# Attention inside one core: the order of TensorE's products, with V-products in groups of three and two, nine P tiles, and seven PSUM banks shared by name

## The chip, the cores and the metric

The kernel runs on one core of one Trainium2 chip. The metric is the device time of one execution in microseconds (us); lower is better. Several executions are timed and the median is given. One execution is also recorded by the hardware profiler; its rows are what this text quotes.

## What is computed

One transformer block for 2048 tokens of width 448: a layer norm with a condition, attention with 16 heads of 28 columns, a residual sum, a second layer norm, and a gated MLP that mixes over tokens. Only the attention matters here:

```python
qkv = (lambda x, *d: x.transpose(*d))((x @ wqkv).reshape(B, S, 3, H, Dh), 2, 0, 3, 1, 4)
q, k, v = qkv[0], qkv[1], qkv[2]
scores = jnp.einsum("bhqd,bhkd->bhqk", q, k) * (Dh ** -0.5)
p = _softmax(scores, axis=-1)
o = jnp.einsum("bhqk,bhkd->bhqd", p, v)
```

with B = 1, S = 2048, H = 16, Dh = 28, all in float32.

## The kernel before

The order of the instructions on each engine is the order in which the code writes them; nothing reorders it later. Tiles come from pools, and an instruction that takes a tile waits until the readers of the tile's last use are done.

A head is worked in 16 key tiles of 128 keys. Three kinds of TensorE (PE) instructions alternate:

- **S products** (`s_mm`, L637): the scores of one key tile against 512 queries, into a PSUM bank; four to a key tile, 64 to a head. ScalarE (ACT) reads each bank and writes the exponential into a P tile (L641). A P tile holds two such results, so a key tile takes two P tiles.
- **M products** (`m_mm`, L607): the same scores laid out the other way, one query tile against 512 keys, 20 tiles (`LEAD`) ahead of the S products. VectorE (DVE) reduces each bank to its row maximum (L612). The maxima of a head are gathered by `m_max` (three small DVE operations, L618, L620, L85), transposed by PE in `m_fin` (L626), copied by DVE (L628), and sent by DMA into two spare rows of the head's queries, so that a later S product already holds the score less its maximum.
- **V products** (`pv_mm`, L652): P times V for one key tile. The four query blocks go to four column strips of the array, into one PSUM bank `o_ps`, the same for a whole head. After the last key tile of a head DVE copies `o_ps` out (`n_copy`, L661); the sums then travel by DMA, DVE takes their reciprocal (L671), and GpSimd (POOL) multiplies.

A slot `u` is one key tile: four S products and four M products in turn, S first. After every second slot come the V products of the two key tiles before. Work of other kinds hangs on slots in a table, `events`: head loads, copies, DMAs, the preparation of weights for later stages (`ws_*`, `wo_*`, `wout_*`). It is issued at the start of its slot.

Of the eight PSUM banks seven are handed out by `bank()`. In the attention loop three of them (tag `s`) belong to S products, four (tag `m`) to M products and to the transpose in `m_fin`; each kind goes round its own banks. The eighth is `o_ps`. Six P tiles go round.

So a stretch of S and M products without V products in between (a *run* below) is 16 products long, and after it PE does the V products of two key tiles (a *group* below).

Of the kernel before, what the change touches and what calls it, by code (L numbers as in the profile page):

```python
# [8 lines left out]
F32 = mybir.dt.float32  # L9
F32R = mybir.dt.float32r  # L10
# [6 lines left out]
S, D, H, DH, FH = 2048, 448, 16, 28, 896  # L17
EPS = 1e-5
SCALE = DH ** -0.5
NT = S // 128  # L20
# [13 lines left out]
def tile_adaln_mha_gmlp(ctx, tc, x, wqkv, wo, w_in, w_spT, b_sp, w_out, cT, w_mod, out):  # L34
    nc = tc.nc
    ctx.enter_context(tc.manual_schedule())
    pe, dve, act, pool, sp = nc.tensor, nc.vector, nc.scalar, nc.gpsimd, nc.sync

    const = ctx.enter_context(tc.tile_pool(name="const", bufs=1))
    dpool = ctx.enter_context(tc.tile_pool(name="dpool", bufs=1, side="right"))  # L40
# [22 lines left out]
    heapD = [dpool.tile([128, n * 896], F32R, name=f"heapD{i}", tag=f"heapD{i}") for i, n in enumerate((8, 8, 4))]  # L63
# [3 lines left out]
    def hview(heap, off, a, b):  # L67
        return heap[:, off : off + a * b].rearrange("p (a b) -> p a b", b=b)
# [3 lines left out]
    class Halves:  # L72


        def __init__(self, n, lo, hi):
            self.n, self.views = n, (lo, hi)
# [7 lines left out]
    def sub(eng, dst, a, hi):  # L84
        eng.tensor_tensor(out=dst, in0=a, in1=hi.bitcast(F32), op=ALU.subtract)  # L85
# [5 lines left out]
    def weight_part(dst, i, raw, hi_eng, lo_eng, zero=True, c0=0):  # L91

        cs = slice(c0, c0 + raw.shape[-1])
        h = dst[:, i if i < 3 else 6, cs]
        if hi_eng is act:
            act.activation(h, raw, AF.Copy)
        else:
            hi_eng.tensor_copy(h, raw)
        if i < 3:
            sub(lo_eng, dst[:, 3 + i, cs], raw, h)  # L100
        else:
            sub(lo_eng, dst[0:64, 7, cs], raw[0:64], h[0:64])
            if zero:
                pool.memset(dst[64:128, 7, cs].bitcast(F32), 0.0)
# [37 lines left out]

    ps = ctx.enter_context(ExitStack())
    ring = ps.enter_context(tc.tile_pool(name="ring", bufs=1, space=PSUM))
    turn = [0]
    ps_o = ps.enter_context(tc.tile_pool(name="ps_o", bufs=1, space=PSUM))

    att = ctx.enter_context(ExitStack())
# [15 lines left out]
    def bank(name, kind=None):  # L164

        if kind is None:
            kind = "smsmsmm"[turn[0] % 7]
            turn[0] += 1
        return ring.tile([128, 512], F32, name=name, tag=kind, bufs=3 if kind == "s" else 4)

    def load_mod(pair, eng):
        for k in range(4):
# [413 lines left out]

    ppool = att.enter_context(tc.tile_pool(name="ppool", bufs=6))

    class Slots:


# [3 lines left out]
            return heapD[n][p, o : o + c.stop - c.start]  # L595

    OT = Slots()
    wos = hview(heapD[2], 0, 8, D)

    pms = {}  # L600

    steady = []

    def m_mm(j, kb):
        h, t = divmod(j, NT)
        mt = bank("mt", *steady)
        pe.matmul(  # L607
            mt, qst[h % 3][:, t * 128 : (t + 1) * 128], kst[h % 3][:, kb * 512 : (kb + 1) * 512], start=True, stop=True
        )
        if h not in pms:  # L610
            pms[h] = npool.tile([128, NT, 4], F32, name="pm")
        dve.tensor_reduce(out=pms[h][:, t, kb : kb + 1], in_=mt, axis=AX.X, op=ALU.max)  # L612
# [3 lines left out]
    def m_max(h):  # L616
        nm = npool.tile([128, NT], F32, name="mxv")
        dve.tensor_reduce(out=nm, in_=pms.pop(h), axis=AX.X, op=ALU.max, negate=True)  # L618
# [4 lines left out]
    def m_fin(h):  # L623
        mx = mxs.pop(h)
        tp = bank("mtp", *steady)
        pe.transpose(tp[0 : 2 * NT, 0:128], mx.bitcast(F32), ident)  # L626
        nf = npool.tile([2 * NT, 128], F32, name="nf", bufs=1)
        dve.tensor_copy(nf, tp[0 : 2 * NT, 0:128])  # L628
# [5 lines left out]
    def s_mm(u, qb):  # L634
        h, kt = divmod(u, NT)
        st = bank("st_ps", "s" if u + LEAD < NU else None)
        pe.matmul(st, kst[h % 3][:, kt * 128 : (kt + 1) * 128], qst[h % 3][:, qb * 512 : (qb + 1) * 512], start=True, stop=True)  # L637
        if qb % 2 == 0:
            ptiles[u, -1] = ppool.tile([128, 2, 512], F32, name="P")
        p = ptiles[u, -1][:, qb % 2, :]  # L640
        act.activation(p, st, AF.Exp, scale=SCALE)  # L641
        ptiles[u, qb] = p
# [4 lines left out]
    def pv_mm(u):  # L647
        h, kt = divmod(u, NT)
        if kt == 0:
            otile[h] = ps_o.tile([128, 512], F32, name="o_ps", tag="o")  # L650
        for qb in range(4):
            pe.matmul(  # L652
                otile[h][32 * qb : 32 * qb + 32, :], V[:, kt, h, :], ptiles.pop((u, qb)), start=kt == 0, stop=kt == NT - 1
            )
# [3 lines left out]
    def n_copy(h):  # L658
        osb[h] = stage.tile([128, 512], F32, name="osb", tag="qf")
        if h < H - 1:  # L660
            dve.tensor_copy(osb[h], otile.pop(h))  # L661
        else:
            act.activation(osb[h], otile.pop(h), AF.Copy)
# [47 lines left out]
    wo_raw = {}  # L711
# [7 lines left out]

    def wo_prep(i):  # L720
        pool.tensor_tensor(out=wo_raw[i], in0=wo_raw[i], in1=bcs["ga"], op=ALU.mult)
        weight_part(wos, i, wo_raw.pop(i), pool, pool)

    wout_t = {}

# [58 lines left out]

    LEAD = 20
    NU = H * NT
    events, late = {}, {}

    def at(slot, fn, *a, when=events):
        when.setdefault(slot, []).append((fn, a))  # L790

    for h in range(H):
        if h >= 2:
            at(h * NT - LEAD - 10, load_head, h)
        e0 = (h + 1) * NT
        at(e0 + 1, n_copy, h)
# [5 lines left out]
        at(h * NT + NT - LEAD, m_max, h)  # L802
        at(max(h * NT + NT - LEAD, -2), m_fin, h, when=late)
# [17 lines left out]

# [20 lines left out]
    steady.append("m")  # L842
    for u in range(NU + 1):
        for fn, a in events.pop(u, []):
            fn(*a)
        j = u + LEAD
        for qb in range(4 if u < NU else 0):
            s_mm(u, qb)
            if j < NU:
                m_mm(j, qb)  # L850
        if u % 2 == 0 and u > 0:
            pv_mm(u - 2)
            pv_mm(u - 1)
        for fn, a in late.pop(u, []):
            fn(*a)
    tail_events = {fn.__name__: [(fn, a)] for k in sorted(events) for fn, a in events[k]}

    def run_tail(*names):
# [23 lines left out]
    def wo_mm(t, steps):  # L882
        if t not in wo_ps:
            wo_ps[t] = bank("wo_ps") if t % 8 < 7 else ps_o.tile([128, 512], F32, name="wo_ps", tag="o")
        for a, b in steps:
            pe.matmul(  # L886
                wo_ps[t][:, :D],
                OT[:, a, t * 128 : (t + 1) * 128],
                wos[:, b, :],
                start=(a, b) == STEPS[0],  # L890
                stop=(a, b) == STEPS[-1],
            )
# [50 lines left out]
    def wo_tile(t):  # L943
        wo_mm(t, STEPS)
        wo_add(t)
# [36 lines left out]
    for t in range(1, HELD):  # L982
        wo_mm(t, STEPS_MAIN)
# [446 lines left out]
```

## Time and profile before

| what | us |
|---|---|
| median of three timed executions | 1400.66 (1400.29 to 1401.11) |
| the profiled execution | 1400.88 |
| its span, first to last instruction | 1399.0 |
| PE busy in it | 1392.6 |
| DVE busy | 1019.4 |
| ACT busy | 774.9 |
| POOL busy | 289.1 |

The span is what the rows describe; 1.9 us of the profiled execution lie outside it. PE runs at its full granted clock throughout. "PE busy" counts a product from the start of its record to its modelled end, and products overlap, so the share of 100% does not tell whether PE loses time. A row of the timeline gives the start, the length, the engine (PEld is PE's loading of weights, which precedes each product), the line, the operation, the number of merged instructions, and in brackets the idle time of the engine before it and what ended it.

### The profile page before, as it was taken

To read this page: it belongs to the slowest core of one execution; us is meant where nothing else is said; L and a number is where in the kernel's file an instruction comes from. 1 tells how busy PE (TensorE), PEld (TensorE's weight loads), DVE (VectorE), ACT (ScalarE), POOL (GpSimd) and SP (SyncE) were. 2 spreads that over 40 slices of the span, in tenths; PEclk is the share of its full clock that TensorE was granted. 3 is DMA by queue.
4 is the path that set the end of the run, shared out by engine and by line. 5 is a ranking of instruction groups with operands and counts; after the bars stand their busy time and mean duration, and the time that the engine had idled before them with its cause. 6 is when DMAs were issued, how large, how long until landed. Compare 5 with 4: busy or idle time off the path is not lost.

```text
span 1399.0 us, 20203 instructions
## 1 busy us (share of the span) xinstructions
PE 1392.6 (100%) x7208; PEld 992.1 (71%) x7208; DVE 1019.4 (73%) x1747; ACT 774.9 (55%) x1491; POOL 289.1 (21%) x275
## 2 busy tenths in 40 slices
PE   9999999999999999999999999999999999999998
PEld 8888655555555555555555555988998888888888
DVE  7788888888888888888888860751356655767473
ACT  5623666677777777666677779363234544434211
POOL 3043212211224143313211231000142430000000
PEclk9999999999999999999999999999999999999999
DMA  9563645555456546654434211534103333446453
GB/s 262 153 194 148 184 116 166 168 162 161 151 168 176 150 164 182 177 161 147 120 94 113 63 50 54 179 115 140 53 0 114 106 112 113 144 136 215 136 177 107
DMA packets 102669, 193.43 MB, mean 138 GB/s; under 512 B 17110, under 2 KB 32086, under 8 KB 100022
## 3 DMA queue, kind: packets, MB, share of 16 engines
q1 hardware_dynamic: 100138, 188.30, 44.4%
q10 hardware_dynamic: 2430, 3.84, 0.7%
q8 instruction: 57, 0.93, 0.3%
q14 instruction: 44, 0.36, 0.1%
HBM read 133.63 MB, written 53.67 MB: 134 GB/s over the span
## 4 chain that ended last, share of the span: by engine, by line
PE 99%; DVE 1%; ACT 0%; issue 0%; POOL 0%; POOLq 0%
PE st_ps L637 18%; PE o_ps L652 17%; PE mt L607 17%; PE acc L1204 6%; PE acc L1206 6%; PE acc L1205 6%; PE z_ps L1130 5%; PE z_ps L1016 5%; PE pq L313 5%; PE wo_ps L886 3%; PE pv L298 2%; PE y_ps L1306 2%; PE y_ps L1305 2%; PE y_ps L1307 2%; PE tp L118 1%; PE wu L240 1%
## 5 line engine op out<-in xcount | busy, mean ns | idle before, releaser
L612 DVE TENSOR_REDUCE pm<-mt 128x1 f32<-128x512 f32 x1024 | 631.0, 680 | 84.4 <-PE mt L607 83.9
L641 ACT ACTIVATE P<-st_ps 128x512 f32<-128x512 f32 x1024 | 514.4, 633 | 205.0 <-PE st_ps L637 205.0
L637 PE MATMUL st_ps<-qst,kst 128*128 128x512 f32 x1024 | 404.2, 406 | 0.2 <-DVE qf L319 0.2
L607 PE MATMUL mt<-kst,qst 128*128 128x512 f32 x1024 | 402.8, 393 | 0.1
L637 PEld LDWEIGHTS st_ps<-qst,kst 128*128 128x128 f32 x1024 | 191.3, 188 | 137.9 <-issue 93.9
L652 PE MATMUL o_ps<-P,V 128*32 128x512 f32 x2048 | 247.1, 598 | 0.0
L607 PEld LDWEIGHTS mt<-kst,qst 128*128 128x128 f32 x1024 | 192.4, 188 | 36.1 <-DVE pm L612 3.1
L780 POOL TENSOR_TENSOR ws_raw<-ws_raw 128x512 f32<-128x512 f32 x80 | 103.0, 1288 | 356.8 <-DMA ws_raw<-in_w_spT_dram 355.0
L1092 ACT ACTIVATE wsp_h<-raw_sp 128x512 fp32r<-128x512 f32 x112 | 70.2, 632 | 162.8 <-PE acc L1206 118.8
L85 DVE TENSOR_TENSOR wsp_l<-raw_sp,wsp_h 128x512 fp32r<-128x512 f32 x112 | 80.5, 729 | 90.6 <-ACT wsp_h L1092 87.8
L652 PEld LDWEIGHTS o_ps<-P,V 128*32 128x32 f32 x2048 | 54.7, 109 | 122.9 <-issue 114.6
L1204 PE MATMUL acc<-wsp_h,heapA 128*128 128x512 f32 x224 | 87.3, 390 | 0.0
L1205 PE MATMUL acc<-wsp_l,heapA 128*128 128x512 f32 x224 | 87.2, 389 | 0.0
L1206 PE MATMUL acc<-wsp_h,heapA 128*128 128x512 f32 x224 | 87.2, 389 | 0.0
L1205 PE MATMUL acc<-wsp_l,heapB 128*128 128x512 f32 x174 | 67.7, 389 | 0.0
L1206 PE MATMUL acc<-wsp_h,heapB 128*128 128x512 f32 x174 | 67.7, 389 | 0.0
L1204 PE MATMUL acc<-wsp_h,heapB 128*128 128x512 f32 x174 | 67.7, 389 | 0.0
L313 PE MATMUL pq<-heapD,heapD 128*128 128x512 f32 x196 | 62.4, 392 | 0.0
L1134 DVE BATCH_NORM_STATS2 stz<-z 128x6 f32<-128x448 f32 x32 | 19.9, 625 | 50.4 <-ACT z L1133 30.0
L1204 PEld LDWEIGHTS acc<-wsp_h,heapA 128*128 128x128 f32 x224 | 42.0, 188 | 8.9 <-DVE cD L1210 0.3
L1206 PEld LDWEIGHTS acc<-wsp_h,heapA 128*128 128x128 f32 x224 | 42.0, 188 | 8.8
L1205 PEld LDWEIGHTS acc<-wsp_l,heapA 128*128 128x128 f32 x224 | 42.0, 188 | 8.6
(219 smaller groups left out, 1595.4 us busy)
## 6 DMA issues: line engine op xcount, KB each, us to landing
ws_raw<-in_w_spT_dram SPq DMA_DIRECT2D x160, 256.0 KB
ws_scr<-ws_raw SPq DMA_DIRECT2D x80, 256.0 KB
raw_sp<-ws_scr SPq DMA_DIRECT2D x80, 256.0 KB
kst<-qk_scr SPq DMA_DIRECT2D x45, 224.0 KB
qst<-qk_scr SPq DMA_DIRECT2D x45, 224.0 KB
raw_sp<-in_w_spT_dram SPq DMA_DIRECT2D x32, 256.0 KB
qk_scr<-qh SPq DMA_DIRECT2D x28, 256.0 KB
qk_scr<-ql SPq DMA_DIRECT2D x28, 256.0 KB
```

The lines of the kernel that those rows point to most:

```text
L85: eng.tensor_tensor(out=dst, in0=a, in1=hi.bitcast(F32), op=ALU.subtract)
L313: pe.matmul(pq, wqk[:, b, m * 128 : (m + 1) * 128], hT[g][:, a, :], start=j == 0, stop=j == NST - 1)
L607: pe.matmul(mt, qst[h % 3][:, t * 128 : (t + 1) * 128], kst[h % 3][:, kb * 512 : (kb + 1) * 512], start=True, stop=True)
L612: dve.tensor_reduce(out=pms[h][:, t, kb : kb + 1], in_=mt, axis=AX.X, op=ALU.max)
L637: pe.matmul(st, kst[h % 3][:, kt * 128 : (kt + 1) * 128], qst[h % 3][:, qb * 512 : (qb + 1) * 512], start=True, stop=True)
L641: act.activation(p, st, AF.Exp, scale=SCALE)
L652: pe.matmul(otile[h][32 * qb : 32 * qb + 32, :], V[:, kt, h, :], ptiles.pop((u, qb)), start=kt == 0, stop=kt == NT - 1)
L780: pool.tensor_tensor(out=a, in0=a, in1=b, op=SUMS[i // 16][2])
L1092: act.activation(hi, raw, AF.Copy)
L1204: pe.matmul(acc[i], zh, hi, start=st == 0, stop=False)
L1205: pe.matmul(acc[i], zh, lo, start=False, stop=False)
L1206: pe.matmul(acc[i], zl, hi, start=False, stop=st == 7)
```

## The change

For the first 14 heads (`GROUPED`) the loop over slots is replaced by a string, `ORDER`, that is run through once a head. It holds 64 `s` (an S product), 64 `m` (an M product), the digits 3, 3, 3, 3, 2 and 2 (V products of so many key tiles), `X` for `m_max`, `F` for `m_fin` and `C` for `n_copy`. S and M products no longer alternate strictly. The 2 near the front does the last two key tiles of the head before. The last two heads keep the old loop.

Every P tile index goes round nine places instead of six: six in the old pool, three in a new tile `p_more` that lies where the weights `wo` were prepared (`heapD2`). So `wo` is prepared later (slots 228 to 246 instead of 120 to 148), and `wout` earlier (120 to 173 instead of 196 to 237).

The seven PSUM banks are tiles with tags `b0` to `b6`. A class `Queue` goes through the same string with fixed durations (nanoseconds, written in the code) and keeps, for each bank, a time at which it counts as free; each product takes the bank that is free first by that count. So a bank can pass from an S product to an M product. Outside the 14 heads the tags `s` and `m` go round banks 0 to 2 and 3 to 6 as before.

```diff
+    p_more = dpool.tile([128, 4 * 896], F32, name="p_more", tag="heapD2")
+    def p_tile(u, half):
+        i = (2 * u + half) % 9 - 6
+        if u >= GROUPED * NT or i < 0:
+            return ppool.tile([128, 2, 512], F32, name="P")
+        return p_more[:, i * 1024 : (i + 1) * 1024].rearrange("p (a b) -> p a b", b=512)
...
+        MM, TURN, PV, PV_IN, PV_OUT, LAG = 230.5, 110, 860, 113, 100, 165
+        TIMES = {"s": (480, 170), "m": (602, 95), "F": (310, 95), "C": (610, 0), "X": (680, 0)}
...
+        def pv(self, n):
+            self.pe += self.PV * n + self.PV_OUT + (0 if self.after_pv else self.PV_IN)
+            self.after_pv = True
+        def work(self, kind, start):
+            eng = "act" if kind == "s" else "dve"
+            self.late[eng] = max(self.late[eng], start) + self.TIMES[kind][0]
+            return self.late[eng] + self.TIMES[kind][1]
...
+        def bank(self, kind):
+            b = min(range(7), key=lambda i: self.free[i])
+            start = max(self.pe, self.free[b])
+            if kind == "F":
+                self.pe = start + self.TURN
+            else:
+                self.pe = start + self.MM + (104 if self.after_pv else 0)
+                self.after_pv = False
+            self.free[b] = self.work(kind, self.pe + self.LAG)
+            return b
...
+    GROUPED = H - 2
+    ORDER = (
+        "ssssmsmsm2Csmsmmsmssmsssmsmmmsmm3msmssmmssmssmmsmsmmsmsmms3smsmssmsm"
+        "ssmmssmmmsmm3smsmsmssmsmsmsmmsssmmX3Fsmsmsmssmmmsmsmssmmsm2smsmsmsmms"
+    )
...
     for i in range(4):
-        at(120 + 8 * i, wo_load, i)
-        at(124 + 8 * i, wo_prep, i)
+        at(228 + 5 * i, wo_load, i)
+        at(231 + 5 * i, wo_prep, i)
...
     for f in range(7):
-        at(196 + 6 * f, wout_raw, f)
-        at(199 + 6 * f, wout_prep, f)
-        at(201 + 6 * f, wout_store, f)
+        at(120 + 8 * f, wout_raw, f)
+        at(123 + 8 * f, wout_prep, f)
+        at(125 + 8 * f, wout_store, f)
...
+    for h in range(GROUPED):
+        n = {"s": 0, "m": 0}
+        for k in ORDER:
+            if k in n:
+                u, qb = h * NT + n[k] // 4, n[k] % 4
...
+                (s_mm if k == "s" else m_mm)(u if k == "s" else u + LEAD, qb, queue.bank(k))
...
+            elif k in "23" and (h or over or n["s"] > 4 * int(k)):
+                for u in range(over, over + int(k)):
+                    pv_mm(u)
+                over += int(k)
+                queue.pv(int(k))
...
+    for u in range(GROUPED * NT, NU + 1):
```

The first place is PE in the middle of a head. A name is out<-in; `mt` is the bank of an M product, `st_ps` of an S product, `o_ps` of the V products; in brackets stands whose count the instruction waits for. Before, a run reads to its end like this, and the V products of two key tiles follow:

```order
L637 MATMUL st_ps<-qst_878,kst_877 128x512 [waits Activation_49]
L607 MATMUL mt<-kst_879,qst_880 128x512 [waits DVE_49]
L637 MATMUL st_ps<-qst_878,kst_877 128x512 [waits Activation_49]
L607 MATMUL mt<-kst_879,qst_880 128x512 [waits DVE_49]
L652 MATMUL o_ps<-P,V 32x512 x8
```

Now the third run of a head (between the first and the second 3 of the string, 12 S and 13 M products) ends like this:

```order
L650 MATMUL mt<-kst_877,qst_878 128x512 [waits Activation_49]
L650 MATMUL mt<-kst_877,qst_878 128x512 [waits DVE_49]
L680 MATMUL st_ps<-qst_876,kst_875 128x512 [waits Activation_49]
L650 MATMUL mt<-kst_877,qst_878 128x512 [waits Activation_49]
L680 MATMUL st_ps<-qst_876,kst_875 128x512 [waits DVE_49]
L650 MATMUL mt<-kst_877,qst_878 128x512 [waits Activation_49]
L650 MATMUL mt<-kst_877,qst_878 128x512 [waits DVE_49]
L680 MATMUL st_ps<-qst_876,kst_875 128x512 [waits Activation_49]
L695 MATMUL o_ps<-P,V 32x512 x6
L695 MATMUL o_ps<-p_more,V 32x512 x6
```

An S product may now wait for DVE and an M product for ACT, and twelve V products stand together instead of eight.

The second place is ACT in the same heads, the exponentials. Before, each waits for PE alone:

```order
L641 ACTIVATE P_2997<-st_ps_2995 128x512 [waits PE_49]
L641 ACTIVATE P_2997<-st_ps_3002 128x512 [waits PE_49]
L641 ACTIVATE P_3010<-st_ps_3008 128x512 [waits PE_49]
L641 ACTIVATE P_3010<-st_ps_3015 128x512 [waits PE_49]
L641 ACTIVATE P_3025<-st_ps_3023 128x512 [waits PE_49]
```

Now many wait for two counts, PE's and ACT's own:

```order
L684 ACTIVATE p_more_1007<-st_ps_2603 128x512 [waits PE_49,Activation_49]
L684 ACTIVATE p_more_1007<-st_ps_2606 128x512 [waits PE_49]
L684 ACTIVATE p_more_1007<-st_ps_2615 128x512 [waits PE_49,Activation_49]
L684 ACTIVATE p_more_1007<-st_ps_2629 128x512 [waits PE_49,Activation_49]
L684 ACTIVATE p_more_1007<-st_ps_2636 128x512 [waits PE_49]
```

A second count is a waiting instruction of its own on ACT's queue ahead of the exponential; there are 570 of these on ACT in the whole program now, and 246 before.

More of the change, by code (lines that the diff above doesn't have):

```diff
@@ L168, in bank @@
             turn[0] += 1
-        return ring.tile([128, 512], F32, name=name, tag=kind, bufs=3 if kind == "s" else 4)
+        if isinstance(kind, str):
+            used[kind] += 1
+            kind = (used["s"] - 1) % 3 if kind == "s" else 3 + (used["m"] - 1) % 4
+        return ring.tile([128, 512], F32, name=name, tag=f"b{kind}")
     def load_mod(pair, eng):
@@ L621, in m_max, with m_fin @@
         sub(dve, mxs[h][:, NT : 2 * NT], nm, mxs[h][:, 0:NT])
-    def m_fin(h):
+    def m_fin(h, b=None):
         mx = mxs.pop(h)
-        tp = bank("mtp", *steady)
+        tp = bank("mtp", b)
         pe.transpose(tp[0 : 2 * NT, 0:128], mx.bitcast(F32), ident)
@@ L721, in wo_prep @@
         pool.tensor_tensor(out=wo_raw[i], in0=wo_raw[i], in1=bcs["ga"], op=ALU.mult)
-        weight_part(wos, i, wo_raw.pop(i), pool, pool)
+        if not wos:
+            heapD[2] = dpool.tile([128, 4 * 896], F32R, name="heapD2", tag="heapD2")
+            wos.append(hview(heapD[2], 0, 8, D))
+        weight_part(wos[0], i, wo_raw.pop(i), pool, pool)
     wout_t = {}
@@ L801, in tile_adaln_mha_gmlp @@
         at(e0 + 9, n_scatter, h)
-        at(h * NT + NT - LEAD, m_max, h)
-        at(max(h * NT + NT - LEAD, -2), m_fin, h, when=late)
+        if not 0 < h <= GROUPED:
+            at(h * NT + NT - LEAD, m_max, h)
+            at(max(h * NT + NT - LEAD, -2), m_fin, h, when=late)
     for c, hl in ((0, 4), (1, 9), (2, 13)):
@@ L840, in tile_adaln_mha_gmlp @@
         qk_unit((m,), g, {j: m_first for j in ((1, 3, 5, 7, 9) if i < 8 else (1, 4, 7, 10))}, last)
-    steady.append("m")
-    for u in range(NU + 1):
+    over = 0
+    for h in range(GROUPED):
[3 more added lines that the diff above has]
+                u, qb = h * NT + n[k] // 4, n[k] % 4
+                if k == "s" and qb == 0:
+                    for fn, a in events.pop(u, []):
+                        fn(*a)
+                n[k] += 1
+                (s_mm if k == "s" else m_mm)(u if k == "s" else u + LEAD, qb, queue.bank(k))
+            elif k == "F":
+                m_fin(h + 1, queue.bank(k))
+            elif k == "X":
+                m_max(h + 1)
+                queue.other(k)
+            elif k == "C" and h:
+                n_copy(h - 1)
+                queue.other(k)
+            elif k in "23" and (h or over or n["s"] > 4 * int(k)):
[3 more added lines that the diff above has]
+                queue.pv(int(k))
+        assert n == {"s": 4 * NT, "m": 4 * NT}, n
+    assert over == GROUPED * NT - 2
+    for u in range(GROUPED * NT, NU + 1):
         for fn, a in events.pop(u, []):
@@ L855, in tile_adaln_mha_gmlp @@
             fn(*a)
+    assert not late
     tail_events = {fn.__name__: [(fn, a)] for k in sorted(events) for fn, a in events[k]}
```

30 lines of the change are left out of this document (18 added, 12 removed).

## The prediction

> **What bounds the kernel now.** I read the chain that ended last first, then PE's timeline inside one run, then DVE's and ACT's beside it, then the places where PE does wait. The page's chain:
>
> ```profile
> PE 99%; DVE 1%; ACT 0%; issue 0%; POOL 0%; POOLq 0%
> ```
>
> and two links of the chain, both the start of a group of V products, 108 groups apart:
>
> ```profile
> 168.03 1.85 PE o_ps L652 x16
> ...
> 788.96 1.85 PE o_ps L652 x16
> ```
>
> PE ends everything, and a run with its group takes (788.96 - 168.03) / 108 = 5.749 us, 45.99 a head. Where that goes shows on PE:
>
> ```profile
> 501.11 0.40 PE L607 MATMUL mt<-kst,qst 128*128 128x512 f32 x1
> 501.43 1.92 PE L652 MATMUL o_ps<-P,V 128*32 128x512 f32 x16
> 503.29 0.50 PE L637 MATMUL st_ps<-qst,kst 128*128 128x512 f32 x1
> 503.62 0.39 PE L607 MATMUL mt<-kst,qst 128*128 128x512 f32 x1
> ...
> 506.87 0.40 PE L607 MATMUL mt<-kst,qst 128*128 128x512 f32 x1
> ```
>
> and on its weight loads:
>
> ```profile
> 501.89 0.13 PEld L652 LDWEIGHTS o_ps<-P,V 128*32 128x32 f32 x4 [0.30 <-issue]
> 502.32 0.13 PEld L652 LDWEIGHTS o_ps<-P,V 128*32 128x32 f32 x4 [0.30 <-issue]
> 503.28 0.19 PEld L637 LDWEIGHTS st_ps<-qst,kst 128*128 128x128 f32 x1 [0.84 <-issue]
> ```
>
> From 503.62 to 506.87 lie 14 products: 0.23 each (0.231 below). The V products advance by 0.43 for four strips (501.89 to 502.32), and a pair of key tiles has four such steps: 0.86 a tile, 1.72 a pair. The rest is the group's own price: 0.09 going in (501.11 to 501.43 is 0.32, not 0.23), 0.14 coming out (501.43 to 503.29 is 1.86, not 1.72), 0.10 for the first product, whose weights were loaded no earlier than the product itself (503.28; the next product starts 0.34 after that load). Sum 0.33, and 16 x 0.231 + 1.72 + 0.33 = 5.75 closes.
>
> How long the readers of the banks take, and how little the banks hold PE up today, stands in the groups of those 108 periods:
>
> ```profile
> L612 DVE TENSOR_REDUCE pm<-mt 128x1 f32<-128x512 f32 x865 | 528.3, 679 | 69.5 <-PE mt L607 69.0
> ...
> L607 PEld LDWEIGHTS mt<-kst,qst 128*128 128x128 f32 x864 | 162.3, 188 | 28.8 <-DVE pm L612 1.7
> ```
>
> A reduce is 0.68 long; the loads of 864 M products waited 1.7 us for DVE in total. DVE in order of time:
>
> ```profile
> 504.05 2.48 DVE L612 TENSOR_REDUCE pm<-mt 128x1 f32<-128x512 f32 x4 [0.87 <-PE mt L607]
> 506.57 0.22 DVE L618 TENSOR_REDUCE mxv<-pm 128x16 f32<-128x64 f32 x1
> ...
> 507.13 2.48 DVE L612 TENSOR_REDUCE pm<-mt 128x1 f32<-128x512 f32 x4
> 509.52 0.27 DVE L628 COPY nf<-mtp 32x128 f32<-32x128 f32 x1
> 509.83 4.87 DVE L612 TENSOR_REDUCE pm<-mt 128x1 f32<-128x512 f32 x8
> ...
> 520.75 0.69 DVE L661 COPY osb<-o_ps 128x512 f32<-128x512 f32 x1 [0.31 <-POOL ws_raw L780]
> 521.36 1.28 DVE L612 TENSOR_REDUCE pm<-mt 128x1 f32<-128x512 f32 x2
> ```
>
> ACT in the same run, and DVE's reciprocals in the whole program (shortest, middle and longest in ns):
>
> ```profile
> 503.82 4.03 ACT L641 ACTIVATE P<-st_ps 128x512 f32<-128x512 f32 x8 [1.72 <-PE st_ps L637]
> ```
>
> ```profile
> L671 DVE RECIPROCAL rt<-rt x15: 239/242/253, 207.5 to 840.8; 128x16 f32<-128x16 f32 x15
> ```
>
> A reduce starts 0.43 after its product (503.62 to 504.05); a reader whose product had its weights loaded late starts 0.54 after that load (503.28 to 503.82). Eight reduces take 4.87, so they follow each other at (4.87 - 0.68) / 7 = 0.60. Eight exponentials take 4.03: at 0.48, with 0.63 to 0.67 for one. DVE's other work in a head is `m_max` 0.56 (506.57 to 507.13), `m_fin` 0.31, `n_copy` 0.61 (520.75 to 521.36) and the reciprocal 0.24; with 64 x 0.60 that is 40.1 of 45.99, and before a run DVE idles 0.87 for want of a product. DVE is nearly as tight as PE.
>
> What a bank that comes late costs PE is seen at the start of the first head, where DVE had extra copies. PE, then the load, then DVE:
>
> ```profile
> 154.85 0.50 PE L607 MATMUL mt<-kst,qst 128*128 128x512 f32 x1
> 155.19 0.40 PE L637 MATMUL st_ps<-qst,kst 128*128 128x512 f32 x1
> 155.45 0.50 PE L607 MATMUL mt<-kst,qst 128*128 128x512 f32 x1
> ```
>
> ```profile
> 154.85 0.19 PEld L607 LDWEIGHTS mt<-kst,qst 128*128 128x128 f32 x1 [0.25 <-DVE pm L612]
> ```
>
> ```profile
> 154.12 3.07 DVE L612 TENSOR_REDUCE pm<-mt 128x1 f32<-128x512 f32 x5
> ```
>
> The first reduce ends at 154.12 + 0.68 = 154.80; the load that waits for it starts at 154.85, its product at once, and the following product 0.34 after the load. Two products take 0.60 there instead of 0.46. A smaller lateness, once in a head, shows the threshold:
>
> ```profile
> 505.24 0.40 PE L637 MATMUL st_ps<-qst,kst 128*128 128x512 f32 x1
> 505.47 0.41 PE L607 MATMUL mt<-kst,qst 128*128 128x512 f32 x1
> 505.72 0.40 PE L637 MATMUL st_ps<-qst,kst 128*128 128x512 f32 x1
> ```
>
> ```profile
> 505.38 0.19 PEld L607 LDWEIGHTS mt<-kst,qst 128*128 128x128 f32 x1 [0.18 <-DVE pm L612]
> ```
>
> The load came 0.14 after the product ahead of it, and from that product to the next but one passed 0.48 instead of 0.46. So the rule I use: **a bank is refilled without loss only if its reader ended 0.05 before the load, and the load is no later than 0.12 after the start of the product ahead (0.12 + 0.34 = 0.46); beyond that PE loses the difference.**
>
> **The change, part by part.**
>
> *Groups.* A head has six groups instead of eight: 2 x 0.33 = 0.67 saved a head, 9.3 us over 14 heads (the first does five instead of seven). The V products themselves, 0.86 a tile, stay.
>
> *Runs.* With six groups a run is 19 to 25 products long instead of 16, and the same seven banks must be emptied and refilled more often before the pause that lets DVE and ACT catch up. Before, count from the first load: product k starts at 0.34 + 0.231 (k - 2); the first M product is the second, its reduce starts at 0.34 + 0.43 = 0.77, and the 16th product takes the bank of the fourth M: read by 0.77 + 3 x 0.60 + 0.68 = 3.25, loadable at 3.30; deadline, the 15th product's start + 0.12, is 3.46. Room: 0.16. That is why nothing waits now.
>
> After, the third run (13 M, 12 S) begins with an M product; I took each bank's turn by replaying the class `Queue`, and each wait by the rule. The j-th M of the run is read by 0.54 + 0.24 (the reciprocal falls here) + 0.60 (j - 1) + 0.68, loadable 0.05 later: 1.51 + 0.60 (j - 1). The 17th product takes the bank of the fifth M: 3.91, deadline 0.34 + 14 x 0.231 + 0.12 = 3.69: 0.22 late. The 19th takes the sixth M's: 4.51 against 4.16, 0.35 in all. The 24th takes the eighth's: 5.71 against 5.31, 0.40 in all. In the fourth and fifth run the 20th product takes the bank of the sixth M, loadable at 0.77 + 3.00 + 0.68 + 0.05 = 4.50 against 0.34 + 17 x 0.231 + 0.12 = 4.39: 0.11. In the second the 15th takes the bank of the fifth S, whose exponential starts at 2.64 (the fourth S is the 8th product, at 1.73; its exponential starts at 2.16, the next 0.48 later): 2.64 + 0.63 + 0.05 = 3.32 against 3.23. The walk over all six runs, with 0.598 for the reduces, gives 0.10, 0.15, 0.41, 0.10, 0.10, 0.10: **0.96 a head**.
>
> That is more than the 0.67 saved: +0.29 a head, 13 heads 3.8, and the first head +0.25 by the same walk: **+4.1 us**. Why the string does not see these waits: its numbers free a bank 480 + 170 after an exponential starts and 602 + 95 after a reduce starts, 0.02 after the record's end, and let the product start then; by the rows above the load comes 0.05 after the end and must lead by another 0.11. By its own count the head loses 0.10.
>
> *P tiles.* Nine instead of six let ACT run further ahead. At the V groups one to six S products beyond the needed ones are issued, and the last tile of a group of three is needed 1.72 after its start, when ACT (0.48 a product) is through: nothing on the path. The extra waits on ACT's queue are 570 - 246 = 324, 23 a head:
>
> ```profile
> L641 ACTq EVENT_SEMAPHORE  x22: 17/17/38, 147.4 to 866.2; - x22
> ```
>
> 23 x 0.017 = 0.4 us of ACT a head, 5.5 in all if nothing covered it, 0 if ACT's 1.7 idle before each run does. I take 0, since ACT has that cover, and keep 5.5 as the upper end.
>
> *F, X, C.* `F` follows a group of three:
>
> ```profile
> 509.05 0.28 PE L626 MATMUL mtp<-ident,mx 128*32 128x128 f32 x1
> 509.09 0.48 PE L637 MATMUL st_ps<-qst,kst 128*128 128x512 f32 x1
> ```
>
> It costs 0.04, before and after. It needs `X` done: by the walk DVE has 2.5 left, `X` included, when the last product before that group starts, and `F` comes 0.32 + 2.58 + 0.14 = 3.0 after that product: 0, and about 0.1 a head if one more reduce stood ahead. The maxima's rows are due at the next head's first S product, 31 products and a group of two later, 9.2 us; 24 products and a group of two, 7.6, were enough for SP's two DMAs behind `F` before. `C` sits on DVE right behind the group that ends a head, as before. SP's queue gets the same DMAs in the same slots but those of `wo` and `wout`.
>
> *`wo`, `wout`.* POOL and SP only: 4 and 7 preparations of three operations change places with their loads and stores, against a POOL that is busy a third of the time in the slots that `wout` goes to (the columns are PE, PEld, DVE, ACT, POOL, clock, DMA share, GB/s):
>
> ```profile
> 500.00:600.00 100.00, 100.00 (x561) 57.77 (x563) 87.93 (x155) 70.53 (x141) 34.02 (x31) 1.00 0.58 173
> ```
>
> ```profile
> L721 POOL TENSOR_TENSOR wo_raw<-wo_raw,bc_ga 128x448 f32<-128x448 f32 x4 | 4.6, 1153 | 0.0
> ```
>
> The first of `wo`'s three operations is 1.15; I take 2.9 for all three. Hidden, 0: no PE, DVE or ACT work of the heads waits for them. Without that cover it would be the last of `wo`, 2.9, since PE takes `wo` after slot 256 and the preparation sits at 246.
>
> Sum: -9.3 + 0.96 x 13 + 0.92 for the first head = +4.1. On the profiled execution 1400.88 that is 1405.0; the median stands 0.2 lower, so 1404.8, rounded to 1405.
>
> **A rule that speaks against this.** The rows say that a load which waits for a bank takes its lead away with it. The Trainium skill, page "TensorE: Matmul & The Clock Gate", section "Architectural detail: the array is 16× 32×32, not 1× 128×128", says that PE's queue is a partial reorder window that can pull weight loads ahead of matmuls in flight. If a load could still make up its lead, 0.11 less would be lost in each run: that is the second rival below. The rows at 154.85 and 505.38 do not show it.
>
> **The rivals.** A measurement of this kernel tells apart about 0.2%, 2.8 us.
>
> 1. *The string's own count holds*: a bank is good 0.02 after its reader ends. Then 0.10 a head is lost: 14 x (0.67 - 0.10) = 8.0 faster, 1392.9. For it: PE lost nothing before. Against it: the loads at 154.85 and after. It decides if loads after a late reader are followed by a product 0.23 later.
> 2. *The lead is not lost.* The six runs lose 0, 0.04, 0.30, 0, 0, 0 (each figure less 0.11): 0.34 a head, 14 x 0.33 = 4.6 faster, 1396.
> 3. *No change that can be told*: DVE and ACT run a little tighter than the walk (0.59 for 0.60 takes 0.07 off the third run and 0.05 off the fourth and fifth), so that 0.5 to 0.85 a head is lost; 1398 to 1403.5.
> 4. *ACT's extra waits are seen*, each exponential that PE waits for comes later: up to 5.5 on top, 1405 to 1410.
>
> **How the numbers follow.** The forecast (1403.5 to 1408) 0.44, rival 1 0.15, rival 2 0.12, rival 3 0.21, rival 4 0.08. Faster 0.27, same 0.21, slower 0.52. The forecast's own range is 1402 to 1409. The range for all reaches down to rival 1's 1393 and up to 1409, and leaves out about half of rivals 1 and 4.
>
> **What would show it.** The group's price: V groups of 24 records instead of 16, 2.7 from first start to the next product. The waits: loads of S and M products with idle time ended by DVE and ACT, followed by a product 0.34 later; about 1 us a head. The period of a head: 46.3; at 45.4 rival 1 holds, at 45.65 rival 2. DVE's idle time before a run grows from 0.87 to about 1.1 or 1.3. I am wrong if PE's products keep 0.23 through the long runs, or if a wait of another kind (P tiles, `F`, the rows of the maxima) stands on the chain.

## The result and the profile after

| | before | after |
|---|---|---|
| median (us) | 1400.76 (1400.29 to 1401.11) | 1415.15 (1414.98 to 1415.97) |
| span of the profiled execution | 1399.0 | 1413.5 |

The ratio is 1.0104, with a 95% interval of 1.0087 to 1.0122. The change makes the kernel 14.4 us slower; the prediction was 4.1 us slower, and 1415 lies outside its range. The sign was right, the size was not.

I read the chain first again. Its shares by engine, from the page of the kernel after:

```profile
PE 96%; DVE 2%; ACT 1%; issue 0%; POOL 0%; ACTq 0%; POOLq 0%
```

PE had 99% before. The share of the other engines says that PE now waits for them; it does not say where. To find the place I cut the span at the first S products of head 0, head 1 and head 14. Those of the kernel before:

```profile
149.95 0.39 PE L637 MATMUL st_ps<-qst,kst 128*128 128x512 f32 x1
...
194.78 0.39 PE L637 MATMUL st_ps<-qst,kst 128*128 128x512 f32 x1
...
792.72 0.39 PE L637 MATMUL st_ps<-qst,kst 128*128 128x512 f32 x1
```

And of the kernel after (the second row merges two products 0.23 apart; head 1 begins with the second, at 202.05):

```profile
156.21 0.40 PE L680 MATMUL st_ps<-qst,kst 128*128 128x512 f32 x1
...
201.82 0.62 PE L680 MATMUL st_ps<-qst,kst 128*128 128x512 f32 x2
...
805.99 0.49 PE L680 MATMUL st_ps<-qst,kst 128*128 128x512 f32 x1
```

So the 14.5 us between the spans fall into four stretches, in us:

| stretch | before | after | difference |
|---|---|---|---|
| start to head 0 | 149.95 | 156.21 | +6.26 |
| head 0 | 44.83 | 45.84 | +1.01 |
| heads 1 to 13 | 597.94 | 603.94 | +6.00 |
| head 14 to the end | 606.28 | 607.51 | +1.23 |

The largest piece lies before the first `s` of the string, where the prediction had nothing at all.

**Ahead of the heads.** In that stage PE makes the queries and keys of the later heads (11 products into one bank, `pq`, which ACT copies out as `qf`) and squeezes single M products in between: the first one behind the first product of a new `pq`, when the `pq` before has only just ended. The list of waits in that stage, after (engine, what waits, for what: total us, times, longest):

```profile
PEld mt L650 <- ACT qf L327: 8.4, 9, 0.9
...
PE mt L650 <- ACT qf L327: 4.6, 9, 0.5
```

The same list before has no such row; nine M products that found a bank now wait for the copy of a `pq`. One of the nine in the timeline:

```profile
89.50 0.39 PE L316 MATMUL pq<-heapD,heapD 128*128 128x512 f32 x1
89.70 0.60 ACT L327 ACTIVATE qf<-pq 128x512 f32<-128x512 f32 x1 [4.81 <-PE pq L316]
...
90.35 0.19 PEld L650 LDWEIGHTS mt<-kst,qst 128*128 128x128 f32 x1 [0.88 <-ACT qf L327]
90.35 0.50 PE L650 MATMUL mt<-kst,qst 128*128 128x512 f32 x1 [0.46 <-ACT qf L327]
...
90.68 0.62 PE L316 MATMUL pq<-heapD,heapD 128*128 128x512 f32 x2
```

The copy ends at 89.70 + 0.60 = 90.30, the load follows 0.05 later. The M product was due at 89.50 + 0.23 = 89.73, so 0.62 is lost, and 0.10 more because the product behind it comes 0.33 after the load. The other eight lose 0.73 to 0.79. Set product against product (both kernels have the same 739 PE products ahead of head 0), the nine places add 6.7 to the kernel before; up to the first of them the kernel after was 0.46 ahead, and that leaves the 6.26.

**In the heads.** Idle time of PE's weight loads, totals over all 1024 loads of each kind; the first row is the S loads before, the other two are both kinds after:

```profile
L637 PEld LDWEIGHTS st_ps<-qst,kst 128*128 128x128 f32 x1024 | 191.3, 188 | 137.9 <-issue 93.9
...
L680 PEld LDWEIGHTS st_ps<-qst,kst 128*128 128x128 f32 x1024 | 191.1, 188 | 113.5 <-DVE pm L655 39.4
L650 PEld LDWEIGHTS mt<-kst,qst 128*128 128x128 f32 x1024 | 189.3, 187 | 81.2 <-DVE pm L655 18.9
```

Before, 3.1 us of the M loads' idle time ended with DVE; now 58 us of both end with DVE. These 58 must not be read as 58 us of new waiting. In the 14 heads 46 of them stand at the first load behind a group, which idles its 0.84 in any case (before, that was put down to issue). Inside the runs of these heads the loads idled 12 us until a reduce of DVE released a bank (50 loads) and 30 us until an exponential of ACT did (150 loads). Inside the runs of heads 1 to 12 of the kernel before it was 1.6 us for DVE and nothing for ACT. `F`, once a head, gives the period without the seams: two of them, six heads apart.

```profile
192.59 0.28 PE L669 MATMUL mtp<-ident,mx 128*32 128x128 f32 x1
...
470.40 0.28 PE L669 MATMUL mtp<-ident,mx 128*32 128x128 f32 x1
```

(470.40 - 192.59) / 6 = 46.30 a head, against 45.99 before and a forecast of 46.28. The third run of one of these heads, on PE and then on its weight loads:

```profile
264.24 0.47 PE L680 MATMUL st_ps<-qst,kst 128*128 128x512 f32 x1
264.55 0.77 PE L650 MATMUL mt<-kst,qst 128*128 128x512 f32 x2
...
264.21 0.19 PEld L680 LDWEIGHTS st_ps<-qst,kst 128*128 128x128 f32 x1 [0.21 <-DVE pm L655]
264.32 0.19 PEld L650 LDWEIGHTS mt<-kst,qst 128*128 128x128 f32 x1
264.81 0.19 PEld L650 LDWEIGHTS mt<-kst,qst 128*128 128x128 f32 x1 [0.30 <-DVE pm L655]
264.92 0.19 PEld L680 LDWEIGHTS st_ps<-qst,kst 128*128 128x128 f32 x1
265.29 0.19 PEld L650 LDWEIGHTS mt<-kst,qst 128*128 128x128 f32 x1 [0.18 <-ACT P L684]
```

Every load that waited is followed by another only 0.10 to 0.12 later. The first waiting load (264.21) went out just ahead of its own product (264.24), and the product behind it starts 0.34 after that load (264.55), as the prediction's rule has it: the lead is lost and paid for. The Trainium skill, page "TensorE: Matmul & The Clock Gate", section "Architectural detail: the array is 16× 32×32, not 1× 128×128", says that weight loads can be pulled ahead of matmuls in flight. These rows do not contradict that, since each load that came late here was waiting for its bank.

The starts of PE's rows also let the two halves of the net be measured apart. What a run loses is the sum of its steps from one product to the next, counted from its second product, less 0.231 a step. What a group costs is the time from the last product ahead of it to the second one behind it, less two such steps and less 0.86 a key tile. Per head, for heads 1 to 6 after and 1 to 12 before:

| | forecast | measured |
|---|---|---|
| lost in the six runs, in order | 0.10, 0.15, 0.41, 0.10, 0.10, 0.10 | 0.08, 0.21, 0.27, 0.12, 0.12, 0.12 |
| their sum | 0.96 | 0.91 |
| saved by two groups fewer | 0.67 | 0.60 (2.69 before, 2.09 after) |
| net | +0.29 | +0.31 |

**Heads 7 to 10.** By the rule heads 1 to 13 should have cost 13 x 0.29 = 3.8; they cost 6.0. Heads 1 to 6 keep to it, head 13 is 0.3 longer (it ends at the seam with the old loop), and heads 7 to 10 are up to 0.7 longer. There POOL prepares `wout` in the very slot in which DVE runs `m_max` before `F`. The timeline after:

```profile
608.29 0.56 POOL L780 CAST wout_h<-wout_l 128x448 fp32r<-128x448 f32 x1
...
608.93 1.14 POOL L85 TENSOR_TENSOR wout_l<-wout_l,wout_h 128x448 fp32r<-128x448 f32 x1
609.12 0.98 DVE L663 CAST mx<-mxv 128x16 fp32r<-128x16 f32 x1
610.13 0.18 DVE L85 TENSOR_TENSOR mx<-mxv,mx 128x16 fp32r<-128x16 f32 x1
610.36 0.09 PEld L669 LDWEIGHTS mtp<-ident,mx 128*32 128x32 f32 x1 [1.32 <-DVE mx L85]
610.36 0.28 PE L669 MATMUL mtp<-ident,mx 128*32 128x128 f32 x1 [0.42 <-DVE mx L85]
```

A DVE cast of 16 columns lasts 0.98 and ends at 610.10, just after POOL's operation (608.93 + 1.14 = 610.07). Before, in all heads, the same casts are 0.175 long. The prediction gave `F` 0.5 of room (3.0 against 2.5); here it waits 0.42; over the whole kernel `F` waits four times, 1.3 in all, and in the kernel before it never does.

### The profile page after: what moved, and what is told of

Its sections match the earlier page's. It is cut to its first block, busy times and chain, and to the rows that moved or that the text cites. A ratio compares the mean times of both kernels' runs of the same rounds, so it can differ in the third digit from the quotient of the medians.

```text
span 1413.5 us, 20506 instructions
## 1 busy us (share of the span) xinstructions
PE 1400.3 (99%) x7208; PEld 985.1 (70%) x7208; DVE 1022.4 (72%) x1747; ACT 779.1 (55%) x1491; POOL 291.5 (21%) x275
## 4 chain that ended last, share of the span: by engine, by line
PE 96%; DVE 2%; ACT 1%; issue 0%; POOL 0%; ACTq 0%; POOLq 0%
PE st_ps L680 17%; PE mt L650 17%; PE o_ps L695 16%; PE acc L1283 6%; PE acc L1284 6%; PE acc L1285 6%; PE z_ps L1209 5%; PE z_ps L1095 5%; PE pq L316 5%; PE wo_ps L965 3%; PE pv L301 2%; DVE pm L655 2%; PE y_ps L1385 2%; PE y_ps L1384 2%; PE y_ps L1386 2%; PE tp L118 1%
## 5 line engine op out<-in xcount | busy, mean ns | idle before, releaser
L684 ACT ACTIVATE P<-st_ps 128x512 f32<-128x512 f32 x728 | 373.5, 627 | 140.6 <-PE st_ps L680 138.8
L650 PE MATMUL mt<-kst,qst 128*128 128x512 f32 x1024 | 372.6, 403 | 4.6 <-ACT qf L327 4.6
L680 PE MATMUL st_ps<-qst,kst 128*128 128x512 f32 x1024 | 364.7, 407 | 1.0 <-DVE qf L322 0.7
L650 PEld LDWEIGHTS mt<-kst,qst 128*128 128x128 f32 x1024 | 189.3, 187 | 81.2 <-DVE pm L655 18.9
L695 PE MATMUL o_ps<-P,V 128*32 128x512 f32 x1456 | 200.2, 597 | 0.0
L684 ACT ACTIVATE p_more<-st_ps 128x512 f32<-128x512 f32 x296 | 155.6, 620 | 68.5 <-PE st_ps L680 67.7
L695 PEld LDWEIGHTS o_ps<-P,V 128*32 128x32 f32 x1456 | 45.8, 109 | 87.1 <-issue 81.5
L695 PE MATMUL o_ps<-p_more,V 128*32 128x512 f32 x592 | 97.7, 597 | 0.0
L1283 PEld LDWEIGHTS acc<-wsp_h,heapA 128*128 128x128 f32 x224 | 42.0, 188 | 9.0 <-DVE cD L1289 0.3
```

What stands on the lines that cost most here:

```text
L650: pe.matmul(mt, qst[h % 3][:, t * 128 : (t + 1) * 128], kst[h % 3][:, kb * 512 : (kb + 1) * 512], start=True, stop=True)
L695: pe.matmul(otile[h][32 * qb : 32 * qb + 32, :], V[:, kt, h, :], ptiles.pop((u, qb)), start=kt == 0, stop=kt == NT - 1)
L1283: pe.matmul(acc[i], zh, hi, start=st == 0, stop=False)
```

## The experiments

"After" is the changed kernel. Each experiment is timed beside the kernel before, whose median was 1400.8 to 1401.1 throughout.

**E1. The old banks ahead of the loop.** Outside the string the tags `b0` to `b2` and `b3` to `b6` are each taken in strict turn. The kernel before also keeps three banks for one kind and four for the other, but its pool gives out in each kind the bank that is released first; its order begins 0203564120353516. E1 puts that order back.

```diff
+    PRE = ("0203564120353516240351624035162403516240531624053162403..." ...)
...
+            n = used["s"] + used["m"] - 1
+            if n < len(PRE):
+                kind = int(PRE[n])
```

> The changed kernel, but the 149 bank choices ahead of the first head's loop are written out as a table that repeats the banks the kernel before had there. Theory A (the 6.3 us lost before the first S product come from naming the banks by a count): first S product back at about 150 us instead of 156.2, time about 1409. Rival B (they come from the nine P tiles' new place or from what is ahead of the heads being scheduled against the loop): first S product stays at 156, time stays at 1415.

Measured: 1407.61, ratio 1.0047 (1.0032 to 1.0062). The first S product:

```profile
150.24 0.63 PE L688 MATMUL st_ps<-qst,kst 128*128 128x512 f32 x2
```

That is 6.0 earlier than after, and the whole is 7.5 us shorter. Most of the rest lies in heads 7 to 10 (0.9) and 14 (0.3), where DVE and POOL now meet at other moments: `F` waits once, 0.42. Heads 1 to 6 stay at 46.25 to 46.31.

**E2. The naming alone.** The kernel before, its order untouched, with strictly named banks everywhere.

```diff
+        used[kind] += 1
+        b = (used["s"] - 1) % 3 if kind == "s" else 3 + (used["m"] - 1) % 4
-        return ring.tile([128, 512], F32, name=name, tag=kind, bufs=3 if kind == "s" else 4)
+        return ring.tile([128, 512], F32, name=name, tag=f"b{b}")
```

> The kernel before with one part of the change alone: the seven banks have names and are taken strictly in turn by a count of each kind, everywhere; order, groups and P tiles are as before. Theory A: the stage before the first head loses the same 6 us and the heads stay at 46.0 us, so about 1407. Rival B (the naming is harmless by itself): 1400.7.

Measured: 1408.42, ratio 1.0053 (1.0038 to 1.0068), 7.3 us slower than the kernel before beside it. First S product and the wait, as in the kernel after:

```profile
156.69 0.39 PE L639 MATMUL st_ps<-qst,kst 128*128 128x512 f32 x1
```

```profile
PEld mt L609 <- ACT qf L326: 8.4, 9, 0.9
```

Its heads keep 45.9 to 46.0: where S and M products alternate, a strict turn costs nothing; where a slow `pq` stands among quick M products, it does. E1 and E2 together settle the largest piece: taken away, the naming gives 6.0 back at the first S product; put alone into the old kernel, it costs 6.7 there.

**E3. POOL's work in other slots.** After, with the `wout` steps four slots earlier and those of `wo` shifted by one to five, so that none stands beside `m_max`.

```diff
-        at(228 + 5 * i, wo_load, i)
-        at(231 + 5 * i, wo_prep, i)
+        at((225, 228, 231, 240)[i], wo_load, i)
+        at((227, 230, 233, 242)[i], wo_prep, i)
...
-        at(123 + 8 * f, wout_prep, f)
+        at(119 + 8 * f, wout_prep, f)
```

> The changed kernel, with the seven preparations of wout four slots earlier and the four of wo at slots 227, 230, 233 and 242, so that none lies in the slot where m_max runs. Theory A (DVE's two small operations of m_max are held up by GpSimd's tensor operations beside them, so the transpose waits): those operations back to 0.18 us in every head, heads 7 to 10 back from 46.5 to 47.0 to about 46.3, two to three us less: 1412 to 1413. Rival B (these heads are slower from DMA load or the longer runs): no change, 1415.

The groups of DVE in 526 to 667 us, first after, then E3:

```profile
L663 DVE CAST mx<-mxv 128x16 fp32r<-128x16 f32 x3 | 1.8, 585 | 0.1
L85 DVE TENSOR_TENSOR mx<-mxv,mx 128x16 fp32r<-128x16 f32 x3 | 1.5, 490 | 0.1
```

```profile
L663 DVE CAST mx<-mxv 128x16 fp32r<-128x16 f32 x3 | 0.5, 174 | 0.1
L85 DVE TENSOR_TENSOR mx<-mxv,mx 128x16 fp32r<-128x16 f32 x3 | 0.5, 174 | 0.1
```

The stretching is gone (mean 585 and 490 ns fall to 174), and heads 7 to 10 take 185.5 instead of 187.0. `F` no longer waits in any head. The profiled span falls by 2.1, but the median only by 0.7, to 1414.48 (ratio 1.0097, 1.0082 to 1.0112), within the scatter of the runs and less than the two to three expected. So the mechanism is shown, its price only bounded: 0.4 (E1 to E4 below) to 0.7 by the medians, 2.1 by the span of the one profiled execution.

**E4. Both.**

> Both repairs together. Theory A says the parts add: 1415.2 - 6.3 - 2.5 = about 1406, which leaves the bank waits of the long runs (0.3 us a head more than the groups save) and the ends of the fixed order. Rival B: what one repair gives is taken back by the other stage, over 1409.

Measured: 1407.18, ratio 1.0045 (1.0028 to 1.0062). Heads 1 to 6 at 46.26 to 46.34. The parts add: 7.5 and 0.7 apart, 8.0 together. What is left over the kernel before is 6.6 by the spans: heads 1 to 12 with about 0.3 each (3.9), head 0 with 1.0, heads 13 and 14 with 1.4, the stage ahead with 0.3.

**H1 and H2. Short maxima.** Is it DVE's hold on the banks that eats the saving of the groups? Two kernels in which DVE holds each M bank 0.26 shorter, because half of the keys are left out of the maxima: the kernel before (H1) and E4 (H2), both with

```diff
-        dve.tensor_reduce(out=pms[h][:, t, kb : kb + 1], in_=mt, axis=AX.X, op=ALU.max)
+        dve.tensor_reduce(out=pms[h][:, t, kb : kb + 1], in_=mt[:, 0:256], axis=AX.X, op=ALU.max)
...
-        act.activation(p, st, AF.Exp, scale=SCALE)
+        act.activation(p, st, AF.Exp, scale=0.25 * SCALE)
```

> The kernel before, with each reduction of an M product reading 256 of its 512 columns, and the exponential scaled by a quarter so that it stays finite: half of the keys are left out of the maxima. DVE is then free much earlier and holds each M bank about 0.3 us less. Theory A (PE bounds the loop of before, its banks are free in time): heads stay at 45.97 us, give or take 0.1, and the whole within 3 us of the kernel before. Theory B (DVE's reading costs the loop of before something too): heads under 45.8. This run is the base for the next one.

> The kernel of experiment e4 (the changed kernel with the old bank choices ahead of the loop and the POOL work moved), with the same half reductions, so half of the keys are left out of the maxima. Theory A (the two products with V saved per head are worth 0.33 us each, and DVE's late reading of the banks between the large groups gives 0.96 us per head back): with DVE early the waits go and heads of 46.27 become 45.3 to 45.4, 0.6 to 0.66 under those of the kernel before in this form; the PE weight loads of the loop show under 10 us of idle time from pm; the whole is 6 to 9 us under the run h1. Theory B (the saved groups are worth little, the weight load of the next product being late for some other reason): heads stay over 45.8. Theory C (ACT's reading holds the banks as well): heads between 45.5 and 45.8, with the waits put down to ACT.

H1: 1400.03, heads 45.96; PE bounds the old loop, as expected. H2: 1403.75, ratio to before 1.0019 (1.0010 to 1.0028), and heads of 46.1, where theory A had 45.3 to 45.4 and the whole 6 to 9 us under H1: a miss for theory A. `F` in H2, 13 heads apart:

```profile
185.78 0.28 PE L677 MATMUL mtp<-ident,mx 128*32 128x128 f32 x1
...
785.25 0.28 PE L677 MATMUL mtp<-ident,mx 128*32 128x128 f32 x1
```

46.11 a head, only 0.2 under E4. The weight loads between 200 and 800 us, first of E4, then of H2:

```profile
L688 PEld LDWEIGHTS st_ps<-qst,kst 128*128 128x128 f32 x829 | 155.5, 188 | 88.5 <-DVE pm L663 36.5 <-issue 10.9 <-ACT P L692 6.7
L658 PEld LDWEIGHTS mt<-kst,qst 128*128 128x128 f32 x831 | 153.7, 187 | 62.7 <-DVE pm L663 17.1 <-ACT P L692 11.1 <-ACT p_more L692 6.3
```

```profile
L688 PEld LDWEIGHTS st_ps<-qst,kst 128*128 128x128 f32 x831 | 155.6, 188 | 86.6 <-issue 43.6 <-ACT P L692 11.3 <-ACT p_more L692 5.5
L658 PEld LDWEIGHTS mt<-kst,qst 128*128 128x128 f32 x834 | 152.9, 188 | 68.6 <-ACT P L692 20.8 <-ACT p_more L692 10.9 <-issue 10.9
```

DVE is no longer named (most of E4's 54 us for DVE are again the 0.84 behind groups). The waits for ACT have grown instead, from 28 us (24 in these rows of E4) to 48. The second and third run still lose 0.21 and 0.27, as in E4; the three behind them fall from 0.12 to 0.04 each. I had changed DVE's time but not the names. `Queue` had fixed the banks for a slow DVE; my reading is that a product is sent to a bank that ACT still reads while one that DVE has left stands free. The walk of the prediction, run with the shorter reduce and each bank chosen as it comes free, gives 45.38. H3 tests that.

**E5. Banks by the walk, order kept.** E4 with a list of bank numbers in place of `Queue`'s choice, made by the prediction's rule; it starts from the state that the stage before leaves (`Queue` starts with all banks free, though DVE is still to read the last `pq`) and goes on through heads 14 and 15.

```diff
+        listed = next(BANKS, None)
+        if listed is not None:
+            kind = int(listed)
```

> The kernel of e4 (old bank choices ahead of the loop, POOL work moved) with the written order ORDER as it is; only the banks of the loop are listed anew: each product takes the bank that is free first, worked out with the durations of the traces, from the state in which the stage before leaves the banks, through the heads 14 and 15 as well. Theory A (the extra time of head 0, +1.0 us, and of head 14, +0.8 us, comes from the bank names at the two seams: the count starts with all banks free, although the last pq of the stage before still holds one, and the plain loop goes round from a phase of its own): head 0 falls from 45.84 to 44.5 to 45.0, head 14 from 43.12 to about 42.3, the 13 heads between stay at 46.23 to 46.30, the whole is 1.5 to 2.5 us under e4, about 1405. Theory B (the extra time at the seams comes from the order, not from the banks): no change, 1407.

Measured: 1405.73, ratio 1.0034 (1.0021 to 1.0047), 1.45 under E4. PE at the start of head 0, in E4 and then in E5:

```profile
150.23 0.63 PE L688 MATMUL st_ps<-qst,kst 128*128 128x512 f32 x2
151.54 0.73 PE L688 MATMUL st_ps<-qst,kst 128*128 128x512 f32 x2 [0.68 <-DVE qf L330]
```

```profile
150.26 1.08 PE L707 MATMUL st_ps<-qst,kst 128*128 128x512 f32 x4
```

The third S product of E4 (and of after) was sent to the bank of the last `pq`; in E5 four follow without a gap. Head 0 falls to 45.28 (less than hoped: it begins with 30 products without a V group, and one S product there still comes 0.6 late, behind ACT), head 14 from 43.12 to 42.33, which is the old 42.29. The heads between stay at 46.3, so with the full reduce the names inside the string were not at fault.

**E6. Another order.** E5 with groups of 2, 2, 3, 2, 3, 2 and 2 key tiles, seven instead of six, and a string in which, by the walk, no bank comes late. The list of banks is made anew for it.

```diff
+    ORDER = (
+        "smmsmsmsssmm2Csmsmsmsmsmsssmssmmm3smsmssmssmsmmmsmm2msmssmmsssmssmsmmm"
+        "3smsmsmssmssmmsmmmss2msmsmsmsssmmXmsmmss2Fsmsmsmsmsmsmmmmssm2smsmsms"
+    )
```

> As the run before it in this list, with another written order: groups of 2, 2, 3, 2, 3, 2, 2 key tiles (seven groups, one more than the change's six), the S and M products between them strung so that neither ACT nor DVE is late for the next bank by the durations of the traces. Theory A (each group is worth 0.33 us, and the change loses on the runs of products that DVE cannot keep up with): a walk by hand gives 45.62 us for each head against 46.23 for the change's order and 45.95 for the kernel before; so heads of 45.6 to 45.75, and the whole 6.5 to 8.3 us under the run before it in this list, about 1397 to 1399, under both kernels. Theory B (the saving of a group is lost anyway, by another limit than the banks): heads stay at 46.0 or over and the whole at or above the kernel before.

Measured: 1398.61 (1398.13 to 1399.48), ratio 0.9985 (0.9976 to 0.9993): 7.1 under E5, 16.5 under the change and 2.2 under the kernel before. `F`, 13 heads apart:

```profile
186.64 0.28 PE L696 MATMUL mtp<-ident,mx 128*32 128x128 f32 x1
...
782.11 0.28 PE L696 MATMUL mtp<-ident,mx 128*32 128x128 f32 x1
```

45.81 a head, a little over the 45.6 to 45.75 expected and the 45.62 of the walk. Heads 4 and 6 take 46.0, the others 45.77 on average; why a run in each of these two loses 0.25 more is open. Measured as in the table above, E6 loses 0.10 a head in its runs where E5 loses 0.94, and pays 0.33 for the group that it gives back: 0.51 a head better. Against the kernel before (45.99) it keeps 0.18.

**H3. Short maxima, banks by the walk.** H2 with the banks listed by the walk for the shorter reduce; the change's order, six groups.

> As h2 (reductions that read half of the columns, so half of the keys are left out of the maxima), with the change's order, but the banks listed by which is free first when DVE is that short. Theory A (what h2 kept, 46.08 us a head, is the bank named for a slow DVE: a product waits for a bank that ACT still reads while another is free): the walk gives 45.38 a head, so 45.4 to 45.6, with head 0 about 43.6 and head 14 about 42.3; the whole 1393 to 1396, 4 to 7 us under h1. Theory B (in long strings of S products ACT itself is the limit, whatever the banks): heads stay at 45.9 to 46.1.

Measured: 1389.80, ratio 0.9923 (0.9909 to 0.9936), 14 us under H2 from the bank numbers alone. Its `F`:

```profile
184.21 0.28 PE L696 MATMUL mtp<-ident,mx 128*32 128x128 f32 x1
...
771.67 0.28 PE L696 MATMUL mtp<-ident,mx 128*32 128x128 f32 x1
```

45.19 a head: 0.77 under H1, 0.59 of it from two groups fewer, the rest because the products inside the runs follow each other at 0.229 instead of 0.231; why, is open. ACT is not the limit; theory B falls. The walk, at 45.38, was too cautious by 0.2 here, which is why the whole came out under the 1393 to 1396 expected.

Set side by side: other bank numbers with the full reduce change nothing inside the heads (E5: 46.32 as in E4), the short reduce with the old numbers gives 0.2 (H2), both together give 1.1 (H3). DVE's hold is what the long runs pay for, and a shorter hold pays only when the banks are named for it.

## Where the prediction was right and wrong

- **The failed step: the naming of the banks was given no term.** The sum has terms for groups and runs inside the heads, and the text ahead of it says that outside them the tags go round "as before". They did not: before, the pool gave out the bank released first; the new names go in strict turn. That is the +6.26 ahead of the heads (6.0 taken away by E1, 6.7 put in by E2), and most of the miss of 10.3. The diff shows it in one line; the order of PE's instructions hides it, since the instructions stay and only whom they wait for changes.
- **First head, +0.25.** Mis-sized: +1.01. The walk started, like `Queue`, with all banks free; E5, which begins from the banks as they are, takes 0.56 of it away.
- **The seam behind the string** had no term either: +1.2 from head 14 on, and 0.3 at the end of head 13. With the banks listed through the seam (E5), head 14 costs 42.33 instead of 43.12, and head 13 46.34 instead of 46.57.
- **`wo` and `wout`, hidden, 0.** The cover was named as "no PE, DVE or ACT work waits for them". True of the data, wrong for the time: POOL's operations hold up DVE's small ones, and `F` waits. 0.4 to 0.7 by medians, up to 2.1 by the profiled span.
- **Group price 0.33.** Right: 0.335 before; after, 0.35, so that two groups fewer save 0.60 and not 0.67 (0.59 from H1 to H3).
- **Waits of 0.96, net +0.29 a head.** The net is right, 46.30 against a forecast of 46.28 where nothing else disturbs, and so is the sum of the waits, 0.91. That they agree so closely is in part luck: the third run was taken 0.14 too long and the second 0.06 too short, and the waits came out lower by about as much as the saving. The rule for a late bank held, and E6 and H3, designed with it, went the way it said, though by the walk E6 should have had 0.2 a head less and H3 0.2 more.
- **The rivals.** 1 needs a late bank to cost no lead and 2 needs the lead to survive a wait; the rows from 264.21 on show that it does not. Rival 3 falls with the 0.91. Rival 4 (ACT's extra waits, up to 5.5 on top) is not needed: the undisturbed heads leave nothing over the forecast waits for it. What would have had to be a rival, a stage outside the heads, was none.

## What to carry to other kernels

When a change renames buffers or replaces a pool by a fixed turn, follow every user of those names through the program, above all a slow one among quick ones, and the states at the seams; the text of the loop that was rewritten is not where it bites. A bank that comes late costs its lateness and the lead of the next weight load, so longer runs between groups pay only while the slower reader keeps up, and a list of banks made for one speed of that reader is wrong for another: H3 gained 14 us over H2 by bank numbers alone. Work on an idle engine is hidden only if its operations do not hold up another engine's.

## What the runs showed of the hardware

DVE's two small operations of `m_max`, which work from SBUF to SBUF, were held up by POOL's elementwise operations: 0.175 alone (E3), 0.53 to 1.12 beside POOL in heads 7 to 10 of the kernel after, and the one shown ended 0.03 after the POOL operation. DVE's reductions out of PSUM keep a mean of 0.68 in that stretch. The Trainium skill, page "GPSIMD Engine Reference", section "1. Specifications", says that POOL shares its SBUF interfaces with VectorE and contends with DVE operations that have two SBUF inputs or run in a two-port mode. The stretched subtraction has two SBUF inputs, so the trace agrees for it; the stretched cast has one, and whether it ran in such a mode no run here shows.
